# Four tokens of q and k to a partition, on half the partitions each, and a new order of all steps

## The chip, the cores and the metric

The kernel runs on one core of one Trainium2 chip. The time is that of one execution on the device, in microseconds (us), and the smaller the better. Before the change it is 206.74 us, the median of three runs that lie between 206.2 and 206.82 us.

## The reference, cut to what matters

Chunked attention over 8 batches, 8 heads, 576 tokens and a head width of 64 is followed by a phase-mixing layer of width 512. Attention stays inside chunks of 64 tokens.

```
q_c, k_c, v_c = (B, H, 9, 64, 64) views of q, k, v
scores = q_c @ k_c^T / 8;  attn = softmax(scores);  x = attn @ v_c     # (8, 576, 512)
theta = x @ w_theta
zr, zi = x * cos(theta), x * sin(theta)
y = einsum('ts,bsd->btd', w_tok_r, zr) + einsum('ts,bsd->btd', w_tok_i, zi)
u = x + y
out = u + max(u @ w_ch, 0)
```

The products with w_tok mix all 576 tokens of a batch, so a row of y needs z of its whole batch.

## The kernel before, in words

The batches are taken in four pairs (p = 0 to 3). A pair has 1152 tokens, cut into five groups: A and B are tokens 0 to 255 and 256 to 511 of its first batch, C and D the same of its second, and M is the 64 last tokens of both. A, B, C and D are "whole" groups of 256 tokens, M has 128.

Each group passes these steps, whose letters stand in the list `ORDER` at the top of the file as letter, optional half of the heads (0 or 1), pair, group, and PSUM banks: `q`, `k`, `v` load (`load_qk`, `load_v`, from the GpSimd queue, since the load turns float32 into float16); `L`, `T`, `N` turn q and k so that the head width lies on the partitions (`qk_t`, transposes on TensorE into PSUM); `tq`, `tk` copy them out of PSUM (`qk_copy`; A is ScalarE, V is VectorE); `S` scores, `e` exponent, `V` attention times v with a column of ones for the sum, `n` division; `X`, `Q` turn x and `xA`, `xV` copy it; `H` is x @ w_theta, `g` cos and sin (with the table loads `pg` and `pe` around it), `z` the two products; `Y` mixes the tokens (`YA`, `YC` and so on take the z of one group at a time), `y` adds x; `U`, `R` turn u, `W` is u @ w_ch, `w` the rest, `s`, `sA` store from the SyncE or ScalarE queue. `lt`, `lw`, `lc` load the weights, `TW` turns the token weights, `D.n` is n products of zeros whose result nobody reads.

The schedule is written out by hand: `tc.manual_schedule()` runs through `ORDER`, and each engine gets its instructions in that order and runs them in that order, waiting where data isn't there. Nothing else reorders the work. The GpSimd loads take turns on eight semaphores, so a load waits until the load eight places before it has landed. The first load of the next pair also waits, through `gate` (line 169), for a recent division.

A whole group of q is loaded by one transfer (line 197) as two tokens to a partition on 128 partitions: for each partition and head it reads two neighbouring tokens, 128 floats, and writes 256 bytes. That is 1024 pieces. k is loaded in the same way beside it. The turning has three forms. `L` ("long") takes 32 transposes of 128 partitions by 64 columns (line 305). `T` ("small") takes 64 transposes of 64 by 64 (line 318), and puts them on the four quadrants of the array. `N` ("plain") serves M. For x and u, `X` and `U` are 8 transposes of 128 by 128 (line 438) for 256 tokens, and `Q` and `R` are 32 of 64 by 64 (line 447).

v is loaded by three transfers for a whole group, one on all partitions and two on half of them (line 221), in pieces of 128 bytes, 2048 in all.

Of the kernel before, what the change touches and what calls it, by code (L numbers as in the profile page):

```python
# [10 lines left out]
FP16 = mybir.dt.float16  # L11
# [10 lines left out]
pg.00 g0.0B H1.0B.0 X1.0A.1 X0.0A.5 xA0.0A xA1.0A n1.0M g1.0B TW.00.3 H0.0A.2 g0.0A n0.0M X.0M.5  # L22
xV.0M TW.01.6 z0.0B H1.0A.5 H.0M.0 twA.01 q.0C z1.0B k.0C L.0C.1.2 twV.00 YB.0A.6 z0.0A g1.0A
z1.0A g.0M tq.0C YA.0A.6 lw.02 z.0M tkA.0C TW.02.0 YM.0A.6 S.0C.2 pe.00 e.0C twV.02 q.1A k.1A
y.0A L.1A.4.5 TW.03.0 tkA.1A q.0D k.0D v.0C L.0D.2.3 tkA.0D tq.1A S.1A.6 e.1A V0.0C.4 v.1A v.0D
lc.00 twV.03 YA.0B.0 V1.0C.6 q.1D n0.0C tq.0D S.0D.2 n1.0C k.1D YM.0B.0 lw.04 U.0A.4 X.0C.5 e.0D
uA.0A V1.0D.6 V0.0D.2 n1.0D YB.0B.0 V0.1A.6 xA.0C n0.0D V1.1A.2 n1.1A n0.1A H.0C.4 W.0A.2 Q.0D.6
y.0B xV.0D T.1D.0 pg.00 g.0C X.1A.4 tkA.1D U.0B.5 w.0A q.1C k.1C z.0C H.0D.6 q.1B xA.1A H.1A.2
uA.0B g.0D W.0B.4 YC.0D.6 g.1A q.1M tq.1D S.1D.0 pe.00 e.1D w.0B k.1B T.1B.4 tkA.1B T.1C.2 z.0D
tq.1C YD.0D.6 tkA.1C k.1M v.1B N.1M.0 TW.04.1 twA.04 YM.0D.6 z.1A S.1C.2 tkA.1M q.2A tq.1B y.0D  # L30
e.1C tq.1M k.2A S.1B.4 v.1D Y.0M.1 v.2A e.1B y.0M T.2A.6 V0.1D.4 V1.1D.2 YC.0C.0 q.2D YM.0C.0
v.1C k.2D tq.2A tkA.2A v.1M S.2A.6 e.2A n0.1D V0.1B.4 n1.1D sA.0A n0.1B V1.1B.2 n1.1B YD.0C.0
y.0C V1.1C.6 S.1M.4 e.1M q.3C X.1D.2 q.2B k.2B q.2M xA.1D X.1B.3 U.0C.0 n1.1C V0.1C.4 V0.1M.1
n0.1M V1.1M.2 q.2C uA.0C k.2C H.1D.6 W.0C.0 n0.1C X.1C.4 xV.1B n1.1M X.1M.5 pg.00 g.1D xA.1C
w.0C H.1B.2 V0.2A.0 v.3M v.2D z.1D xA.1M n0.2A q.3D g.1B V1.2A.6 n1.2A H.1M.4 g.1M z.1B U.0M.5
H.1C.0 uA.0M v.3D g.1C Q.2A.6 T.2B.2 z.1M Y.1A.4 q.3A z.1C Y.1D.0 tkA.2B xA.2A tq.2B Y.1C.2 k.3C
y.1D y.1A y.1C S.2B.0 pe.00 e.2B T.2C.6 T.2D.4 tq.2C tkA.2D tkA.2C v.2M k.3A R.0D.2 tq.2D k.2M
Y.1B.0 uA.0D v.2C v.2B N.2M.2 V0.2B.6 q.3M y.1B tkA.2M tq.2M S.2D.4 e.2D k.3D n0.2B Y.1M.3
S.2M.0 V1.2B.4 n1.2B S.2C.6 W.0M.2 e.2M V1.2M.0 e.2C Q.2B.4 xA.2B y.1M w.0M s.0M V0.2M.1 n0.2M
H.2A.6 R.1A.4 n1.2M V1.2C.0 H.2B.2 q.3B uV.1A pg.00 g.2A n1.2C Q.2M.0 xV.2M T.3D.4 tq.3D R.1B.6  # L40
W.1A.0 g.2B H.2M.2 s.0B z.2A v.3C s.0C w.1A s.1A uA.1B z.2B k.3B U.1C.3 W.0D.6 g.2M W.1B.0 uA.1C
tkA.3D w.0D s.0D z.2M V1.2D.2 w.1B sA.1B R.1D.6 n1.2D uA.1D Y.2A.4 S.3D.6 V0.2D.0 W.1D.2 y.2A
pe.00 e.3D R.1M.4 n0.2D uV.1M w.1D T.3B.0 tkA.3B tq.3B Q.2D.6 Y.2B.4 xA.2D v.3B V0.2C.6 S.3B.0
y.2B n0.2C H.2D.2 sA.1D k.3M e.3B V0.3B.0 n0.3B V1.3B.4 n1.3B W.1C.6 w.1C X.2C.0 pg.00 g.2D
W.1M.1 T.3C.2 w.1M xA.2C Q.3B.4 V0.3D.6 H.2C.0 tkA.3C n0.3D N.3M.6 xA.3B tq.3C g.2C H.3B.4 g.3B
z.2D tq.3M R.2B.2 tkV.3M z.2C V1.3D.0 n1.3D z.3B Y.2C.6 y.2C S.3M.0 uA.2B S.3C.2 pe.00 e.3M
# [13 lines left out]
def kernel(  # L60
# [186 lines left out]
    def cast_theta(a, copy):  # L247
        copy(out=wtheta16[:, 2 * a : 2 * a + 2], in_=wraw[a])
# [35 lines left out]
    def qk_t(p, g, f, form, *banks):  # L284
        n = 1 if g == "M" else 2
        ne, e0 = part(f)
        t = nats[p, g]
        if form != "small":

            if n == 2:  # L290
                pss = [psum(b, 1, FP16)[:, 0 : ne * n * P] for b in banks]
# [35 lines left out]
    def qk_copy(p, g, f, which, how):  # L327
        ps = st[p]["ps_qkT", g, f][which]
        _, nx, n, c = ps.shape
        name = "qk"[which] + "T"  # L330
        t = tmp.tile([P, nx, n, c], FP16, name=name, tag=f"{name}{n}")
# [12 lines left out]

    def scores(p, g, f, bank):
# [7 lines left out]
        for cc in range(n):  # L353
            for e in range(ne):
                for h in range(2):
                    for r in range(2):
                        x, r0 = (r * ne + e, 0) if form == "small" else (e, r)
                        k0 = (n * r0 + cc) * CH
                        i0 = r0 * CH + cc * CH // 2
                        kc = kf[half[h], x, k0 : k0 + CH]  # L360
                        if n == 1 or form == "plain":
# [4 lines left out]
                        nc.tensor.matmul(ps[to], kc, qc)  # L366
        st[p]["ps_sT", g, f] = ps

    def exps(p, g, f):
# [8 lines left out]
            )  # L378
            return
        if st[p]["form", g, f] != "plain":  # L380
            ps = ps.rearrange("p x (s i) -> p x i s", s=2)
        nc.scalar.activation(  # L382
            out=eT.rearrange("p h r e c -> p (h r e) c"), in_=ps, func=AF.Exp, scale=scale
        )
# [314 lines left out]
    def store(p, g, f, queue):  # L699
# [112 lines left out]
```

## Time and profile before

| what | value |
|---|---|
| median of three runs | 206.74 us |
| the profiled execution's own time | 205.98 us |
| its span | 204.2 us |
| TensorE (PE) busy | 192.3 us, 94% |
| VectorE (DVE) busy | 126.0 us, 62% |
| ScalarE (ACT) busy | 115.6 us, 57% |
| GpSimd (POOL) busy | 89.3 us, 44% |
| queue of the GpSimd loads | 81264 packets, 16.01 MB |

The span is what the profile covers; 1.8 us of the execution lie around it. "PE" rows are products and transposes, "PEld" the weight loads that run beside them. A row's time before an instruction is idle time of its engine, and the name behind the arrow is what ended it; "issue" means that the profile shows nothing that the engine waited for.

### The profile page before, as it was taken

The page shows a single profiled execution, that of the slowest core. Times are in us where ns is not written, and L with a number is a line of the kernel's source. Part 1 is how long each engine was busy: PE and PEld are TensorE (multiplying, and loading weights), DVE is VectorE, ACT ScalarE, POOL GpSimd, SP SyncE. Part 2 cuts the span into 40 slices and gives each one's busy share as a digit, 9 for nine tenths or more (in the row PEclk, how much of TensorE's full clock was granted, in tenths as well). Part 3 has the DMA queues.
Part 4 walks back from the last instruction along what each step waited for, and adds up shares of the span by engine and source line. Part 5 has one row for each costly group of instructions (what it writes and reads, how often), then busy time and mean ns, then how long its engine had stood idle before and what let it go on. Part 6 is the DMA issues. An engine that isn't in the chain of part 4 may idle for free.

```text
span 204.2 us, 7908 instructions
## 1 busy us (share of the span) xinstructions
PE 192.3 (94%) x3584; PEld 102.8 (50%) x3584; DVE 126.0 (62%) x226; ACT 115.6 (57%) x142; POOL 89.3 (44%) x130
## 2 busy tenths in 40 slices
PE   7977999999997799999999999999999999999991
PEld 2344556656464365544654645445555544454440
DVE  0335696667364587924467886589666768643662
ACT  2044996678985378960759836498960857030120
POOL 7889495649989289999403502230400000000000
PEclk9999999999999999999999999999999999999997
DMA  6999999999999989999904993940723002042546
GB/s 210 144 150 150 179 190 169 146 181 118 169 170 157 114 158 176 167 173 159 122 11 127 214 256 135 157 27 3 51 59 106 3 3 104 0 167 108 190 177 185
DMA packets 87009, 27.00 MB, mean 132 GB/s; under 512 B 80064, under 2 KB 81984, under 8 KB 86976
## 3 DMA queue, kind: packets, MB, share of 16 engines
q0 software_dynamic: 81264, 16.01, 93.2%
q1 hardware_dynamic: 3920, 7.08, 10.2%
q10 hardware_dynamic: 1792, 3.41, 4.6%
q8 instruction: 28, 0.46, 0.9%
q14 instruction: 5, 0.04, 0.0%
HBM read 33.06 MB, written 9.44 MB: 208 GB/s over the span
## 4 chain that ended last, share of the span: by engine, by line
PE 76%; DMA 13%; POOL 5%; issue 4%; DVE 0%; DVEq 0%; POOLq 0%
PE ps L564 29%; PE ps L478 27%; DMA v<-in_v_dram 7%; DMA qk<-in_k_dram 4%; PE ps L550 4%; PE ps L438 3%; PE ps L318 3%; PE ps L400 3%; PE ps L447 3%; POOL qk L197 3%; PE ps L366 2%; DMA out_dram<-o 1%; POOL v L221 1%; POOL wnat L232 1%; PE ps L301 1%
## 5 line engine op out<-in xcount | busy, mean ns | idle before, releaser
L564 PE MATMUL ps<-z,wT 128*128 128x512 f16 x288 | 65.6, 380 | 1.5 <-issue 1.5
L564 PEld LDWEIGHTS <-wT 128*128 128x128 f16 x288 | 26.9, 98 | 32.6 <-issue 1.8
L221 POOL DMA_DIRECT2D v<-in_v_dram x48 | 36.2, 766 | 7.0 <-DMA qk<-in_k_dram 3.3
L683 DVE TENSOR_TENSOR x<-ps,x 128x1024 f16<-128x1024 f32 (+1 forms) x22 | 22.5, 1028 | 25.2 <-PE ps L564 22.4
L478 PE MATMUL ps<-wtheta,xT 128*128 128x512 f16 x144 | 34.4, 380 | 0.1
L478 PE MATMUL ps<-wch,uT 128*128 128x512 f16 (+1 forms) x148 | 34.1, 374 | 0.0
L382 ACT ACTIVATE eT<-ps 128x1024 f16<-128x1024 f32 (+1 forms) x18 | 16.6, 928 | 25.8 <-PE ps L366 24.4
L693 DVE SCALAR_TENSOR_TENSOR o<-ps,x 128x1024 f32<-128x1024 f32 (+2 forms) x23 | 22.5, 990 | 10.7 <-PE ps L478 6.6
L461 ACT COPY uT<-ps 128x1024 f16<-128x1024 f16 (+1 forms) x16 | 14.4, 909 | 25.5 <-PE ps L447 12.5
L414 DVE TENSOR_TENSOR x<-ps,recip 128x512 f16<-128x512 f32 (+1 forms) x40 | 25.5, 638 | 1.4
L338 ACT COPY kT<-ps 128x1024 f16<-128x1024 f16 (+1 forms) x18 | 16.4, 927 | 15.9 <-PE ps L305 10.8
L492 ACT ACTIVATE cos<-ps,pihalf 128x1024 f16<-128x1024 f32 (+1 forms) x22 | 21.2, 965 | 6.1 <-PE ps L478 3.5
L169 POOL COPY seen<-recip 1x1 f32<-1x1 f32 x13 | 2.7, 210 | 45.9 <-DVE recip L412 45.9
L478 PEld LDWEIGHTS <-uT 128*128 128x128 f16 x148 | 13.7, 98 | 15.0 <-issue 0.4
L478 PEld LDWEIGHTS <-xT 128*128 128x128 f16 x144 | 12.9, 98 | 13.8 <-issue 0.2
L496 ACT ACTIVATE sin<-ps 128x1024 f16<-128x1024 f32 (+1 forms) x22 | 19.2, 873 | 0.0
L334 DVE COPY qT<-ps 128x1024 f16<-128x1024 f16 (+2 forms) x23 | 12.9, 569 | 6.4 <-PE ps L305 4.4
L197 POOL DMA_DIRECT2D qk<-in_q_dram x16 | 14.5, 905 | 2.3 <-issue 1.5
L412 DVE RECIPROCAL recip<-ps 128x8 f32<-128x8 f32 (+1 forms) x40 | 7.9, 197 | 12.2 <-PE ps L400 10.3
L197 POOL DMA_DIRECT2D qk<-in_k_dram x16 | 14.4, 900 | 1.0 <-issue 0.6
L137 ACT ACT_TABLE_LOAD x11 | 14.1, 1283 | 0.2
L461 ACT COPY xT<-ps 128x1024 f16<-128x1024 f16 (+1 forms) x13 | 11.8, 922 | 1.3 <-PE ps L447 1.0
(52 smaller groups left out, 204.5 us busy)
## 6 DMA issues: line engine op xcount, KB each, us to landing
qk<-in_q_dram POOLq DMA_DIRECT2D x16, 256.0 KB, 6.4
qk<-in_k_dram POOLq DMA_DIRECT2D x16, 256.0 KB, 6.5
out_dram<-o SPq DMA_DIRECT2D x8, 512.0 KB, 3.6
out_dram<-o ACTq DMA_DIRECT2D x6, 512.0 KB, 3.3
v<-in_v_dram POOLq DMA_DIRECT2D x40, 64.0 KB, 5.5
v<-in_v_dram POOLq DMA_DIRECT2D x16, 128.0 KB, 6.2
wraw<-in_moe_w_theta_dram SPq DMA_DIRECT2D x2, 512.0 KB, 3.8
out_dram<-o SPq DMA_DIRECT2D x8, 128.0 KB, 2.3
```

The costliest lines, as they stand in the source:

```text
L197: nc.gpsimd.dma_start(t.rearrange("p (h x) -> p h x", h=H)[:, hs], ap[2 * p + bb, :, s0 : s0 + GT, :].rearrange("h (p s) d -> p h (s d)", ...
L221: nc.gpsimd.dma_start(v16[rows, slot + tile, :, 0:D], v[2 * p + bb, :, t0 : t0 + m, :].rearrange("h s d -> s h d"),)
L338: nc.scalar.copy(out=t.rearrange("p x s c -> p x (s c)").rearrange("p x (c s) -> p x c s", s=2), in_=ps.rearrange("p x s c -> p x c s"),)
L382: nc.scalar.activation(out=eT.rearrange("p h r e c -> p (h r e) c"), in_=ps, func=AF.Exp, scale=scale)
L414: nc.vector.tensor_tensor(out=tokens(p, g, "x")[:, :, f * NE * D : (f + 1) * NE * D].rearrange("p c (h d) -> p c h d", h=NE), in0=psv[:, 0 ...
L461: (nc.vector.tensor_copy if how == "V" else nc.scalar.copy)(out=to.rearrange("p b (r c) -> p b r c", c=CH), in_=psv)
L478: nc.tensor.matmul(ps[:, a * DM : a * DM + cols.stop - cols.start], xT[:, b0 + a, db, :], weight[:, db, cols], start=(db == 0), stop=(db = ...
L492: nc.scalar.activation(out=cos[:, 0:n].rearrange("p a e -> p (a e)"), in_=pin, func=AF.Sin, bias=pihalf, scale=1.0,)
L496: nc.scalar.activation(out=sin[:, 0:n].rearrange("p a e -> p (a e)"), in_=pin, func=AF.Sin)
L564: nc.tensor.matmul(ps[:, a * DM : a * DM + DM], wT[:, kt, t0 : t0 + P], zs[bb], start=(done + k == 0), stop=(done + k == NK - 1),)
L683: nc.vector.tensor_tensor(out=u, in0=ps, in1=u, op=ALU.add)
L693: nc.vector.scalar_tensor_tensor(out=o, in0=ps[:, 0 : n * m].rearrange("p (j d) -> p j d", j=n), scalar=0.0, in1=u, op0=ALU.max, op1=ALU.add,)
```

## The change

Whole groups of q and k are loaded with four neighbouring tokens to a partition: q of the group on partitions 0 to 63, k on partitions 64 to 127 of the same tile. A piece is then 256 floats in and 512 bytes out, and a group of q has 512 pieces in place of 1024, and k the same. Two new forms of turning go with it. `F` ("four") takes 64 transposes of 64 by 64 on the four quadrants, for q and k together. `FL` ("four long") takes 32 transposes of 128 partitions by 64 columns, each of which turns q and k of one head at once. M is loaded as before. The copy of q may now run on ScalarE too (`tqA`). The copy of k puts its tokens back in natural order, and the scores pick q in steps, four at a time.

The whole list `ORDER` is new. In pair 0 the groups come as C, B, A, D, M instead of B, M, A, C, D; q and k of all groups and v of C are loaded ahead of the other v, and the token weights `lw` behind all of it. For whole groups, `L` in five groups (two of them by halves of the heads) and `T` in eleven become `FL` in six groups (two by halves) and `F` in ten; M of pair 0 is turned by `L` in place of `N`. `Q` and `R` (small) give way to `X` and `U` in part. The table loads `pe` and `pg` go from 11 to 7. The products of zeros go from 42 to 43, 26 of them ahead of the first transpose instead of 31.

```diff
 ORDER = """
-q.0B k.0B init.00 D.12.0 lt.00 ctV1.00 ctV0.00 q.0M k.0M id.00 D.19.0 L0.0B.0.1 tkA0.0B
-L1.0B.7.6 tq1.0B N0.0M.5 tkV0.0M tkA1.0B q.0A N1.0M.1 tq0.0B S1.0B.6 tkV1.0M tq0.0M D.3.2
-S0.0M.2 e1.0B tq1.0M S0.0B.4 v.0B D.4.0 V1.0B.0 e0.0B e0.0M V0.0B.2 n0.0B k.0A S1.0M.6 D.4.5
-L1.0A.5.4 v.0M n1.0B L0.0A.3.2 tq1.0A e1.0M Q0.0B.0 tq0.0A tkA1.0A S1.0A.6 Q1.0B.4 tkA0.0A
-S0.0A.2 e1.0A e0.0A V1.0M.6 xV1.0B v.0A V0.0M.7 xV0.0B V1.0A.0 n1.0A V0.0A.4 lw.00 n0.0A H0.0B.2
...
+qF.0C kF.0C init.00 qF.0B kF.0B lt.00 id.00 D.12.0 D.14.0 F.0C.0.1 tqA.0C D.4.2 FL0.0B.2 tq0.0B
+tkA.0C S.0C.0 tkA0.0B FL1.0B.6 e.0C qF.0A ctV0.00 S0.0B.4 kF.0A tkA1.0B FL0.0A.2 v.0C tq0.0A
+qF.0D tq1.0B D.5.0 V1.0C.0 tkA0.0A e0.0B S0.0A.2 n1.0C V0.0C.4 FL1.0A.6 n0.0C D.3.0 X.0C.0 e0.0A
+tqA1.0A q.0M xV.0C tkA1.0A S1.0B.2 e1.0B S1.0A.6 e1.0A kF.0D FL.0D.4 tkA.0D k.0M L1.0M.0 tq1.0M
+L0.0M.1 tkV0.0M ctA1.00 v.0B tqA0.0M v.0A tkV1.0M tq.0D D.5.6 S.0D.6 V0.0B.4 V1.0B.2 S1.0M.0
+e1.0M e.0D v.0D V0.0A.0 n0.0B V1.0A.4 n1.0B n0.0A S0.0M.6 e0.0M n1.0A H.0C.2 X1.0A.0 lw.00
+xV1.0A v.0M X0.0A.1 V0.0D.4 xV0.0A lw.02 pg.00 g.0C V1.0D.6 H1.0A.0 g1.0A H0.0A.1 TW.00.2 qF.1C
...
 def load_qk
+        if plain is None:
+            t = nats[p, g][half[which]].rearrange("p a x -> p (a x)")
+            nc.gpsimd.dma_start(
+                t.rearrange("p (h x) -> p h x", h=H),
+                (q, k)[which][2 * p + bb, :, s0 : s0 + GT, :].rearrange(
+                    "h (p s) d -> p h (s d)", s=4
+                ),
+            )
+            return
...
 def qk_t
+        if form == "four":
+            t = t.rearrange("p a x -> p (a x)")
+            pss = [psum(b, 1, FP16)[:, 0 : ne * 4 * CH] for b in banks]
+            pss = [ps.rearrange("p (e s c) -> p e s c", e=ne, s=4) for ps in pss]
+            for e in range(ne):
+                for s in range(4):
+                    for w in range(2):
+                        for h in range(2):
+                            x0 = ((2 * (e0 + e) + h) * 4 + s) * D
+                            nc.tensor.transpose(
+                                pss[w][half[h], e, s],
+                                t[half[w], x0 : x0 + D],
+                                id16[half[w], half[w]],
+                            )
+        elif form == "four long":
+            form = "four"
+            t = t.rearrange("p a x -> p (a x)")
+            ps = psum(banks[0], 2, FP16)[:, 0 : ne * 4 * P]
+            ps = ps.rearrange("p (e s w c) -> p e s w c", e=ne, s=4, w=2)
+            for e in range(ne):
+                for s in range(4):
+                    for h in range(2):
+                        x0 = ((2 * (e0 + e) + h) * 4 + s) * D
+                        nc.tensor.transpose(
+                            ps[half[h], e, s].rearrange("p w c -> p (w c)"),
+                            t[:, x0 : x0 + D],
+                            id16,
+                        )
+            pss = [ps[:, :, :, w] for w in range(2)]
...
 def qk_copy
-        elif n == 1 or st[p]["form", g, f] == "plain":
+        elif which == 0 or n == 1 or st[p]["form", g, f] == "plain":
             nc.scalar.copy(out=t, in_=ps)
...
-                    "p x (c s) -> p x c s", s=2
+                    "p x (c s) -> p x c s", s=n
...
 def scores
+                        if form == "four":
+                            k0 = (2 * r + cc) * CH
+                            kc = kf[half[h], e, k0 : k0 + CH]
+                            qc = qT[half[h], e, :, k0 // 4 : k0 // 4 + CH // 4]
...
 parted = {
+        "qF": lambda p, g, f: load_qk(p, g, 0, None, f),
+        "kF": lambda p, g, f: load_qk(p, g, 1, None, f),
+        "F": lambda p, g, f, *banks: qk_t(p, g, f, "four", *banks),
+        "FL": lambda p, g, f, *banks: qk_t(p, g, f, "four long", *banks),
+        "tqA": lambda p, g, f: qk_copy(p, g, f, 0, "A"),
```

More of the change, by code (lines that the diff above doesn't have):

```diff
@@ L23 @@
[L23 to L46, printed above, removed]
@@ new lines @@
+e.2M y.1C S.2B.6 F.2C.2.3 tkA.2C tq.2C Y.1M.0 y.1M X.2A.5 S.2C.2 V0.2M.4 sA.0B v.2C e.2B kF.3B
+xA.2A n0.2M V0.2B.0 W.0C.6 V1.2M.4 n0.2B H.2A.0 e.2C w.0C s.0C V0.2D.2 n1.2M V1.2B.4 n1.2B
+W.1A.6 X.2M.4 n0.2D pg.00 g.2A v.3D xA.2M X.2B.0 w.1A V0.2C.2 xA.2B F.3B.1.5 tq.3B V1.2C.6 n1.2C
+n0.2C U.1C.4 U.1B.0 uV.1B X.2D.1 tkA.3B xA.2D H.2M.5 v.3M v.3B H.2B.6 g.2M W.1B.0 g.2B kF.3A
+uV.1C R.1D.2 uA.1D Q.2C.4 H.2D.6 xA.2C z.2A z.2M W.1C.2 s.1A k.3M z.2B g.2D w.1C H.2C.4 s.1C
+W.1D.2 g.2C w.1B F.3C.0.1 F.3A.4.5 w.1D z.2C tkA.3A S.3B.6 e.3B tq.3A Y.2B.2 tq.3C tkA.3C z.2D
@@ L56 @@
+R.2C.4 s.2B z.3D R.2D.6 uA.2D z.3C Y.3M.0 y.3B R.3B.2 R.3A.6 uA.3A w.2M Y1.3C.1 uV.3B s.1D y.3M
+W.2D.2 Y0.3C.0 y1.3C uA.2C y0.3C W.3A.4 U1.3C.0 W.2C.6 w.2D s.2D sA.2M U.3M.1 w.2C sA.2C W.3B.2
+w.3A sA.3A w.3B Y1.3D.7 y1.3D Y0.3D.4 sA.2A y0.3D uA.3M W.3M.1 w.3M uA1.3C R0.3C.6 R0.3D.4
+uV0.3C s.3B R1.3D.2 uA0.3D W1.3C.0 W0.3D.1 s.3M w1.3C s1.3C w0.3D s0.3D uA1.3D W1.3D.7 w1.3D
+s1.3D W3.3C.0 W2.3C.1 w3.3C sA3.3C w2.3C sA2.3C
 """.split()
@@ L287, in qk_t @@
         t = nats[p, g]
-        if form != "small":
+        if form == "four":
[27 more added lines that the diff above has]
+            pss = [ps[:, :, :, w] for w in range(2)]
+        elif form != "small":
             if n == 2:
@@ L330, in qk_copy @@
         name = "qk"[which] + "T"
-        t = tmp.tile([P, nx, n, c], FP16, name=name, tag=f"{name}{n}")
+        t = tmp.tile([P, nx, n, c], FP16, name=name, tag=f"{name}{min(n, 2)}")
         st[p][name, g, f] = t
@@ L359, in scores @@
                         i0 = r0 * CH + cc * CH // 2
-                        kc = kf[half[h], x, k0 : k0 + CH]
-                        if n == 1 or form == "plain":
+                        if form != "four":
+                            kc = kf[half[h], x, k0 : k0 + CH]
+                        if form == "four":
+                            k0 = (2 * r + cc) * CH
+                            kc = kf[half[h], e, k0 : k0 + CH]
+                            qc = qT[half[h], e, :, k0 // 4 : k0 // 4 + CH // 4]
+                        elif n == 1 or form == "plain":
                             qc = qf[half[h], x, k0 : k0 + CH]
@@ L380, in exps @@
         if st[p]["form", g, f] != "plain":
-            ps = ps.rearrange("p x (s i) -> p x i s", s=2)
+            s = 4 if st[p]["form", g, f] == "four" else 2
+            ps = ps.rearrange("p x (s i) -> p x i s", s=s)
         nc.scalar.activation(
```

31 lines of the change are left out of this document (21 added, 10 removed).

## The prediction

> **What bounds the kernel now.** First the page's busy times, then the chain of waits, which is PE at 76%. So I read TensorE's idle places.
>
> ```profile
> span 204.2 us, 7908 instructions
> PE 192.3 (94%) x3584; PEld 102.8 (50%) x3584; DVE 126.0 (62%) x226; ACT 115.6 (57%) x142; POOL 89.3 (44%) x130
> ...
> q0 software_dynamic: 81264, 16.01, 93.2%
> ...
> q8 instruction: 28, 0.46, 0.9%
> ```
>
> PE is full from 20 us on, but for one place. Its instructions in order of time show the start and that place (the bracket is idle time and its end):
>
> ```profile
> 1.20 8.28 PE L277 MATMUL ps<-zeros 128*128 128x512 f16 x31 [1.20 <-DVE pihalf L131]
> ...
> 10.85 0.86 PE L305 MATMUL ps<-id,qk 128*64 128x128 f16 x24 [0.96 <-DMA qk<-in_k_dram]
> ...
> 20.48 0.84 PE L400 MATMUL ps<-v,eT 64*64 64x65 f16 x48 [0.44 <-ACT eT L382]
> ...
> 63.06 0.29 PE L366 MATMUL ps<-qT,kT 64*64 64x64 f16 x13 [1.29 <-issue]
> ...
> 68.17 2.10 PE L564 MATMUL ps<-z,wT 128*128 128x512 f16 x9 [1.52 <-issue]
> ```
>
> The first 20 us go by the loads: PE works off zeros until q of the first group is in, and is idle for k. The two "issue" gaps are code. The trace has 28 reads of 16,384 bytes on the instruction queue, 256 instructions each; one begins at 60.6, the next at 65.8, and PE goes on 2.4 us after each begins, 128 matmuls apart. While loads fill the queues, 4.2 to 6.5 us pass from PE's entry into one such block until the next can run; PE had 4.1 and 3.7 us of work in these two blocks.
>
> Stretches with mostly one kind of load give the rates (last column: GB/s read and written, here written):
>
> ```profile
> 5.00:20.00 15.00, 12.35 (x248) 6.80 (x247) 5.66 (x14) 4.17 (x9) 13.15 (x19) 1.00 1.80 148
> 36.00:38.00 2.00, 1.88 (x82) 1.45 (x77) 0.95 (x2) 1.39 (x3) 1.63 (x3) 1.00 2.34 154
> 40.20:42.00 1.80, 1.80 (x52) 1.42 (x51) 0.83 (x3) 1.80 (x3) 1.50 (x3) 1.00 1.21 199
> 43.50:45.00 1.50, 1.50 (x38) 0.84 (x38) 0.89 (x4) 0.97 (x2) 0.00 (x0) 1.00 1.74 177
> ```
>
> 36 to 38 us is v (128-byte pieces), 43.5 to 45 q and k (256), 40.2 to 42 w_ch (1024): 154, 177 and 199 GB/s. The first column after the stretch is PE.
>
> **PE's own work.** Spacing from start to start, from the chain of waits:
>
> ```profile
> 65.42 0.64 PE ps L318 x64
> ...
> 75.19 3.56 PE ps L478 x16
> ...
> 81.14 0.38 PE ps L400 x32
> ...
> 85.35 11.76 PE ps L564 x54
> ...
> 98.60 0.27 PE ps L447 x32
> ...
> 162.88 0.55 PE ps L438 x8
> ```
>
> With 0.1 us for a change of tile shape (32 small ones take 0.27 or 0.38 us), that is 8.4 ns for a 64x64 transpose, score or attention product, 216 for 512 columns, 56 for a 128x128 transpose; L305's 32 take 1.0 us up to the next instruction, 31 each. Counts in both programs, by these prices:
> - 64x64 of q and k 704 to 640: -0.54 us
> - 64x64 of x and u 672 to 480: -1.61
> - 128x128 of x and u 120 to 168: +2.68
> - 128x64 of q and k 160 to 208: +1.49
> - 128x128 of M 32 to 24: -0.45
> - zeros 42 to 43: +0.22
> - changes of tile shape 95 to 99: +0.40
>
> Sum **+2.2 us**, all on PE: before's order adds up to 188.3 us, the new one to 190.5. The new forms have no row; I price them by L318 and L305, whose operand shapes they share. Should all 64x64 of `F` need a change of shape more per group, 10 x 0.1 = 1.0 comes on top; a gain from them I bound by 0.5.
>
> **What PE loses.** Before's last matmul ends at 199.6 (195.99 + 3.64), so 199.6 - 188.3 = 11.3 us are lost: 7.3 by 26.2 us (clock still low for the first six zeros 1.3, start 1.2, the loads and latencies the rest), 3.4 between 57 and 74 (2.8 are the two gaps), 0.6 later. From the last matmul to the end of the span, 4.6 us, nothing changes: four last columns, two stores.
>
> **The new start.** The queue's order decides. Before, the last piece of v of A landed at 20.8 us by the trace. Up to it 1.05 MB of q and k (5.9 us at 177 GB/s) and 0.92 MB of M and v (6.0 at 154) pass: 11.9 us, after a first packet at 4.7. So 4.2 us are lag: the last of the 16 engines ends about 2 us behind the middle one, and starts and landings cost the rest. In the new order v of A stands behind q and k of four groups (2.10 MB), M's (0.26) and v of C and B, with A's 0.79. The 0.26 + 0.79 take 6.8 us at 154. The 512-byte pieces have no row: their rate lies between 177 and 199, so 11.9 to 10.5 us; I take 190 (as close to one as to the other), 11.05. Then v of A is in at 4.7 + 17.9 + 4.2 = **26.8 us** (26.2 to 27.6 by the rate; 28.9 if the lag grows with the work; 25.0 if it shrinks to what it is at 50 us, under 0.5 from middle to last).
>
> PE reaches V0.0A with 16.9 us of order behind it: 43 zeros 9.29, 64 transposes of `F.0C` 0.54, 64 + 32 of `FL` 2.98, 16 of M 0.50, 136 scores 1.14, 64 attention products 0.54, X.0C 0.45, about 15 changes 1.5. So 26.8 - 16.9 = **9.9 us** are lost there, if what comes earlier is in time: F.0C about 10.4 (before's k at 10.85, the same bytes, issues 0.2 to 0.4 us shorter), FL0.0B 13, FL0.0A 16.5, FL.0D 22, none later than V0.0A needs. The zeros count as work in both orders.
>
> **Code in the new start.** PE's blocks 94 to 222, 222 to 350 and 350 to 478 matmuls hold only 3.9, 3.9 and 4.2 us. The block entered near 18.6 lets the next run at 22.8 to 25.1, that one the next at 27.7 to 31.6; PE wants them about 23.5 and 29.4. I take 0.4 here. The later blocks under load hold 9.7, 5.8, 7.9, 5.0, 5.8 and 7.6 us against 4.2 to 6.5, so I take 0.5 in place of before's 2.8. (The blocks with 3.5 and 4.4 us come past 110 us; there the trace shows 2 to 4 us from entry to readiness.)
>
> The Trainium skill, "Runtime: NRT & Kernel Launch", section "Instruction fetch mechanics", says that crossing a 16 KiB boundary is mostly hidden. The two gaps say that under load it is not; by the rule the 0.9 us here would go, and the sum be 207.9.
>
> **The rest.** POOL issues a q or k in 0.90 us; the same count of pieces (512) for half of v takes 0.68, so 32 x 0.22 = 7 us leave POOL, which idles 46 us at its gates: nothing. Loads of pair 1 stand 2 to 3 us ahead of PE by the same rates, so they cost nothing unless PE is 3 us early. ACT loses four table loads (4 x 1.28 + 4 x 0.2 = 5.9 us) and swaps copies with DVE one for one; both are under 62% and cost nothing, except that from H.0C on ACT has 12.4 us in a row (three pairs of cos and sin, two wT copies of 1.16, the table) that PE needs 13.5 us later: cover 1 us, and 1 us lost if it goes. SP carries only theta in the first half of the run, in both orders; moved stores have the same bytes and, but for the last two columns, a later one behind them.
>
> **Sum.** Lost: 9.9 + 0.4 + 0.5 + 0.3 at the end = 11.1 against 11.3, -0.2; work +2.2. That is +2.0 on the profiled execution (205.98), 208.0; the median stands 0.76 above it, so **208.8 us**.
>
> **Rivals.**
> - Wide pieces are fast (faster). Place: the first 25 us. If 512-byte pieces write faster than 199 GB/s, v of A comes earlier; from 258 GB/s on, 11.05 becomes 8.15 and the loss falls by 2.9, which beats the 2.2 of work and 0.6. At twice 190, PE waits for code next (pair 350 not before 22): loss 8, time 205.6. Against it: w_ch at 1024 bytes reaches 199, reading twice that in float32, and the first 2 us of the theta load, which isn't turned to float16, read and write 393.
> - The Trainium skill, "DMA: Bandwidth & Descriptors", section "Specifications", asks for 512 bytes at least for line rate, and names a read-modify-write below. By it this change would bring just that rival's gain; the rows show a slope of size alone, 154 to 177 to 199, and no step.
> - Code holds the start (slower still): each of the three short blocks takes 6.5 us from 11.6 on, so matmul 478 comes at 31.6 instead of 29.8: +1.8, 210.6, plus the ACT chain 211.6. For it: the block entered at 19.6 in before took 6.5.
> - Half of the partitions is slow (slower): at v's 154 GB/s the 2.10 MB take 13.6, +2.6: 211.4. Against it: at 36 to 38 us pieces for half and for all partitions pass at one rate.
> - The start doesn't matter (same): lag shrinks to 25.0, code is hidden: -1.8 - 0.9, 206.1 to 206.9.
>
> **Numbers.** Likeliest (207.4 to 210.0) 0.46; code 0.18; half partitions 0.08; same or nearly 0.14; wide pieces 0.10; the order's unseen waits, above 211, 0.04. A measurement here tells 0.3%, 0.6 us, from no change. Faster: 0.10 and half of the 0.14 = 0.17; same 0.11; slower 0.72. Range 205.8 to 211.5.
>
> **What would show it.** Right: PE busy about 2 us up with zeros alike; first transposes near 10.4 us; V0.0A near 27; gaps "issue" at 61 to 68 gone; DMA at 5 to 25 us writing 150 to 180 GB/s. Wrong: GB/s well above 200 there, or PE working without a break before 25 us; or "issue" gaps at 24 and 30 us that the sum has at 0.4.

## The result and the profile after

| | before | after |
|---|---|---|
| median of 9 runs of each | 206.74 us (205.49 to 207.67) | 208.1 us (207.44 to 209.07) |
| the profiled execution | 205.98 us | 207.44 us |
| its span | 204.2 us | 205.3 us |
| start of the last matmul | 199.35 us | 201.29 us |
| from there to the end of the span | 4.86 us | 4.04 us |

The changed kernel is slower, by less than 2%: the ratio is 1.0153, 95% interval 1.0119 to 1.0187, and the ratio of the medians is 208.1 / 206.74 = 1.0066. The first leaves out executions more than 1.5% above the quickest of their kernel and implies a mean of about 205.0 us for before (208.1 / 1.0153), less than the quickest of the nine in the table, so the medians are the safer measure of the size. Both are given below. 208.8 us was predicted.

The page's first lines, after:

```profile
span 205.3 us, 7582 instructions
...
PE 194.4 (95%) x3417; PEld 105.1 (51%) x3417; DVE 123.7 (60%) x223; ACT 114.8 (56%) x139; POOL 81.5 (40%) x128
```

PE does 167 matmuls fewer and is busy 2.1 us longer (192.3 before): the fewer and larger transposes cost more than the small ones that they replace.

PE's instructions in order of time, after, are to be compared with the same view of before. The bracket is idle time and what ended it:

```profile
1.19 7.37 PE L287 MATMUL ps<-zeros 128*128 128x512 f16 x26 [1.19 <-DVE pihalf L131]
...
9.67 0.69 PE L308 MATMUL ps<-id,qk 64*64 64x64 f16 x62 [0.96 <-DMA qk<-in_k_dram]
...
12.45 0.64 PE L323 MATMUL ps<-id,qk 128*64 128x128 f16 x16 [1.11 <-DMA qk<-in_k_dram]
...
14.22 0.32 PE L412 MATMUL ps<-qT,kT 64*64 64x64 f16 x16 [0.19 <-ACT kT L379]
15.32 0.64 PE L323 MATMUL ps<-id,qk 128*64 128x128 f16 x16 [0.78 <-DMA qk<-in_k_dram]
...
17.51 0.29 PE L447 MATMUL ps<-v,eT 64*64 64x65 f16 x13 [0.21 <-DMA v<-in_v_dram]
...
19.47 0.23 PE L412 MATMUL ps<-qT,kT 64*64 64x64 f16 x5 [1.58 <-issue]
...
23.69 0.24 PE L346 MATMUL ps<-id,qk 128*64 128x128 f16 x1 [0.26 <-issue]
...
26.44 0.62 PE L447 MATMUL ps<-v,eT 64*64 64x65 f16 x32 [0.55 <-ACT eT L422]
27.36 0.26 PE L412 MATMUL ps<-qT,kT 64*64 64x64 f16 x8 [0.29 <-ACT eT L429]
```

Three more rows of before belong beside those that the prediction shows:

```profile
12.00 0.27 PE L301 MATMUL ps<-id,qk 128*128 128x128 f16 x2 [0.29 <-DMA qk<-in_q_dram]
12.85 0.49 PE L301 MATMUL ps<-id,qk 128*128 128x128 f16 x6 [0.58 <-DMA qk<-in_k_dram]
...
19.57 0.22 PE L366 MATMUL ps<-qT,kT 64*64 64x64 f16 x4 [0.82 <-issue]
```

After, PE waits for three k loads (2.85 us together) and briefly for v (0.21), twice for code (1.84) and three times for ScalarE (1.03). Before, the start has 1.83 us of waits for loads, 0.82 for code and 0.44 for ScalarE. The last two waits for ScalarE are for PSUM banks, by the kernel's own list: `V0.0A` writes a bank that the exponent of M's scores has to read first, and the scores after it take the banks of group D's. The code gaps of before at 63 and 68 us have no counterpart: between 60 and 70 us PE is never idle. The stretches, after (the first column after the stretch is PE, the last GB/s read and written):

```profile
8.00:14.00 6.00, 3.93 (x135) 2.38 (x133) 0.88 (x2) 2.35 (x3) 2.76 (x5) 1.00 1.50 185
...
60.00:70.00 10.00, 10.00 (x156) 5.20 (x153) 7.84 (x16) 3.79 (x5) 3.62 (x7) 1.00 1.07 111
```

Set against the order's work at the prediction's prices, PE had lost 9.5 us when `V0.0A` began and 10.2 at `H.0C`, and 10.9 at the last matmul (201.29 - 190.4). Before had lost 7.2 at 26 us, 10.6 at 68 us and 11.1 at the end (199.35 - 188.2). So the change pays 3.0 us more at the start (1.2 for loads, 1.0 for code and 0.6 for ScalarE by the rows above), saves about as much later, and its 2.2 us of added work remain, less 0.8 us of a shorter end.

### The profile page after: what moved, and what is told of

It is laid out like the page before. It is cut to its first block, busy times and chain, and to the rows that moved or that the text cites. A ratio compares the mean times of both kernels' runs of the same rounds, so it can differ in the third digit from the quotient of the medians.

```text
span 205.3 us, 7582 instructions
## 1 busy us (share of the span) xinstructions
PE 194.4 (95%) x3417; PEld 105.1 (51%) x3417; DVE 123.7 (60%) x223; ACT 114.8 (56%) x139; POOL 81.5 (40%) x128
## 4 chain that ended last, share of the span: by engine, by line
PE 88%; DMA 8%; issue 2%; ACT 1%; DVE 0%; DVEq 0%; POOLq 0%
PE ps L611 31%; PE ps L525 31%; PE ps L485 5%; DMA v<-in_v_dram 4%; PE ps L597 4%; PE ps L447 3%; DMA qk<-in_q_dram 3%; PE ps L412 3%; PE ps L308 2%; PE ps L494 2%; PE ps L323 2%; PE ps L276 2%; PE ps L287 1%; PE ps L342 1%; ACT eT L429 0%
## 5 line engine op out<-in xcount | busy, mean ns | idle before, releaser
L525 PE MATMUL ps<-wtheta,xT 128*128 128x512 f16 x144 | 33.9, 379 | 0.0
L508 ACT COPY uT<-ps 128x1024 f16<-128x1024 f16 (+1 forms) x11 | 8.9, 818 | 22.9 <-PE ps L494 9.5
L525 PEld LDWEIGHTS <-xT 128*128 128x128 f16 x144 | 13.2, 98 | 14.3
L375 DVE COPY qT<-ps 128x1024 f16<-128x1024 f16 (+2 forms) x14 | 7.7, 561 | 16.0 <-PE ps L323 13.3
L459 DVE RECIPROCAL recip<-ps 128x8 f32<-128x8 f32 (+1 forms) x40 | 7.8, 195 | 10.9 <-PE ps L447 10.9
L377 ACT COPY qT<-ps 128x1024 f16<-128x1024 f16 (+2 forms) x9 | 7.7, 852 | 11.2 <-PE ps L308 8.2
L508 ACT COPY xT<-ps 128x1024 f16<-128x1024 f16 (+1 forms) x12 | 10.7, 910 | 5.5 <-PE ps L485 5.1
L169 POOL COPY seen<-recip 1x1 f32<-1x1 f32 x11 | 2.2, 198 | 27.9 <-DVE recip L459 27.9
L180 POOL DMA_DIRECT2D qk<-in_q_dram x16 | 11.1, 695 | 4.5 <-issue 1.0
L287 PE MATMUL ps<-zeros 128*128 128x512 f16 x43 | 11.7, 424 | 1.2 <-DVE pihalf L131 1.2
```

The costliest lines, as they stand in the source:

```text
L287: nc.tensor.matmul(psum(bank, 1), zeros[:, 0:P], zeros)
L508: (nc.vector.tensor_copy if how == "V" else nc.scalar.copy)(out=to.rearrange("p b (r c) -> p b r c", c=CH), in_=psv)
L525: nc.tensor.matmul(ps[:, a * DM : a * DM + cols.stop - cols.start], xT[:, b0 + a, db, :], weight[:, db, cols], start=(db == 0), stop=(db = ...
```

## The experiments

Each kernel was timed in five rounds beside the kernel before on the same chip. In the first four the median of before was 206.9 us, in the next four 206.1, and in the last four 206.28 (runs 9 and 10), 205.91 and 207.07, so kernels of different groups are compared by their ratios. "Work" is the order's matmuls at the prediction's prices, "lost" the start of the last matmul less the work up to it.

**1. The changed kernel again**, as the reference for its variants.

> The changed kernel itself, beside the parts below. Theory (work and start): TensorE has 2.2 us more work, loses about as much at the start and at code as before in all; 1 to 3.5 us over before, ratio 1.005 to 1.017. Rival (the loads themselves cost, half of the partitions each): the same here; it is told apart by the two next kernels.

Measured: 208.83 us (207.96 to 210.44), ratio 1.0196 [1.0121, 1.0271], ratio of medians 1.0093. The profiled execution lost 11.4 us; V0.0A began at 26.85 us; code gaps of 1.19 and 0.54 us stand at 19.6 and 24.1 us, after the same matmuls as in the first trace. The picture repeats to half a microsecond.

**2. The loads alone**: before's order, with the four-token loads and the two new forms.

```diff
-q.0B k.0B init.00 D.12.0 ... L0.0B.0.1 tkA0.0B L1.0B.7.6 ...   T.1D.0   T.1B.4   T.1C.2   T.2A.6
+qF.0B kF.0B init.00 D.12.0 ... FL0.0B.0 tkA0.0B FL1.0B.6 ...   F.1D.0.1 F.1B.4.5 F.1C.2.3 F.2A.6.7
```

> The order of before, with the four-token loads and their transposes in it and nothing else changed. Theory (work and start): the same count of transposes at the same prices, so no more work; a q or k passes in 1.36 to 1.40 us instead of 1.45, the first k lands about 1.2 us earlier than before, and the two code gaps at 61 to 68 us stay, shortened at most: 0 to -1.5 us against before, ratio 0.993 to 1.000. Rival (the loads cost): the loss of the change shows here, ratio 1.01 or more.

Measured: 207.61 us (205.94 to 208.81), 1.0118 [1.0041, 1.0195], medians 1.0034. The theory's gain is not there: 7.1 us were lost by 26 us, as in before. PE's instructions and the stretches of this run:

```profile
63.24 0.31 PE L412 MATMUL ps<-qT,kT 64*64 64x64 f16 x15 [1.54 <-issue]
68.89 0.21 PE L447 MATMUL ps<-v,eT 64*64 64x65 f16 x1 [2.34 <-issue]
```
```profile
30.00:56.00 26.00, 25.71 (x483) 14.99 (x482) 16.42 (x29) 19.96 (x22) 16.51 (x26) 1.00 1.46 147
56.00:80.00 24.00, 20.12 (x549) 11.53 (x548) 14.09 (x27) 12.78 (x17) 15.01 (x23) 0.93 1.38 135
```

The two code gaps grew from 2.8 to 3.9 us. The granted clock (the column ahead of the last two) has a mean of 0.93 in the stretch that holds them: it was 0.50 from 69.75 to 73.16 us, just behind the longer gap, and 1.00 around that, which makes 3.41 x 0.5 = 1.7 us more. The profiled execution is the longest of the six. Three of them have a mean clock of 0.981 to 0.990 and took 208.2 to 208.8 us, the other three 0.997 to 1.000 and 205.9 to 207.0. So the loads by themselves gain nothing where before's order wants them, and the loss of this execution is code and clock. The rival got the ratio, though not that of the medians, and not by slow loads on half of the partitions.

**3. The order alone**: the changed order with two-token loads (`F` to `T` or `L`, `FL` to `L`).

```diff
-qF.0C kF.0C init.00 qF.0B kF.0B lt.00 id.00 D.12.0 D.14.0 F.0C.0.1 tqA.0C D.4.2 FL0.0B.2
+q.0C k.0C init.00 q.0B k.0B lt.00 id.00 D.12.0 D.14.0 T.0C.0 tqA.0C D.4.2 L0.0B.2.3
```

> The new order with the loads and transposes of before (two tokens to a partition; L or T where FL or F stood). Theory (work and start): 2.2 us more work as in the change, and v of group A comes later by eight loads of some 0.08 us and by the 2.2 us that half the pieces saved at the landing of the first ones, 1 to 2 us in all: ratio 1.012 to 1.025. Rival (the loads cost): with the old loads the loss goes, ratio 1.000 to 1.005.

Measured: 210.09 us (209.21 to 211.53), 1.0246 [1.0186, 1.0306], medians 1.0154, as the theory had it. PE's instructions, run 3:

```profile
11.48 0.45 PE L358 MATMUL ps<-id,qk 64*64 64x64 f16 x32 [1.06 <-DMA qk<-in_k_dram]
...
27.68 0.42 PE L446 MATMUL ps<-v,eT 64*64 64x65 f16 x29 [0.70 <-DMA v<-in_v_dram]
```

The first k is worked on at 11.5 us instead of 9.7, and V0.0A waits for v itself, at 27.7 us. Work is 191.2 us (0.7 more), 13.2 us are lost (11.4 in run 1). No gap of this start is put down to code: PE reaches matmul 222 at 19.46 us, just when the changed kernel's code let it go on (19.47). The clock was 0.50 from 12.1 to 15.5 us. The four-token form is worth 1.3 us in the new order (210.09 - 208.83), of which 0.7 is TensorE's work and not the loads', and nothing in the old one.

**4. Without 17 products of zeros** (`D.4.2`, `D.5.0`, `D.3.0`, `D.5.6` left out; nobody reads their results).

> The changed kernel without the 17 products of zeros that stand between the first steps of pair 0 (the 26 ahead of them stay); the result does not depend on them. Theory (the start goes by the loads and the code): the 3.7 us of zeros only fill waiting; the time is that of the change within 0.7 us. Rival (the start goes by TensorE's queue): 2.5 to 3.7 us less than the change, ratio about 0.998 to before. If the idle places lower the clock instead, it is slower than the change by up to 2 us.

Measured: 209.0 us (207.87 to 209.63), 1.0189 [1.0136, 1.0242], medians 1.0101. Work fell by 4.0 us to 186.5 and the time did not. The stretches:

```profile
15.00:20.00 5.00, 2.92 (x71) 2.30 (x71) 2.18 (x6) 2.45 (x5) 3.55 (x5) 0.65 1.93 173
20.00:25.00 5.00, 3.82 (x119) 3.50 (x119) 2.07 (x5) 3.55 (x6) 4.94 (x8) 0.67 1.93 120
25.00:30.00 5.00, 4.15 (x108) 2.03 (x95) 3.31 (x8) 3.24 (x6) 4.55 (x8) 0.67 1.23 139
```

Run 1, the middle one of these stretches:

```profile
20.00:25.00 5.00, 4.46 (x111) 3.21 (x112) 2.50 (x7) 4.43 (x7) 5.00 (x8) 1.00 1.95 122
```

The zeros fill time that PE would wait for loads and code anyway, so taking them out removes no waiting; and without them the granted clock from 15 to 30 us is about 0.66, where run 1 has 1.00. It is no chance of one execution: the mean clock of this run's six executions is 0.975 to 0.982, that of run 1's 0.984 to 1.000.

**5. Before's order, four-token loads, less code**: run 2 with `FL` for `F` in groups 1B, 1C and 2A, 96 matmuls fewer.

```diff
-F.1B.4.5 ... F.1C.2.3 ... F.2A.6.7
+FL.1B.4  ... FL.1C.2  ... FL.2A.6
```

> The order of before with the four-token loads, and three of its groups (B and C of pair 1, A of pair 2, those turned between 56 and 66 us) turned by 32 wide transposes (FL) instead of 64 small ones (F): 96 matmuls and 96 weight loads fewer there, three quarters of a code block, for 3 x 0.45 = 1.35 us more work. Theory (code, and the clock after it): the gaps of 1.5 and 2.3 us between 61 and 69 us go or shrink under 1 us in all and the clock stays full there, so 1 to 3.5 us less than the loads alone, 204.5 to 206.5. Rival (the gaps are waits for loads that the profile doesn't show): the gaps stay and the work comes on top, 1 to 1.5 us more than the loads alone.

Measured: 207.23 us (205.88 to 211.17), 1.0067 [1.0025, 1.0108], medians 1.0055. The profiled execution is the longest of the twelve, so its places are read and not its sizes. PE's instructions:

```profile
85.14 0.19 PE L307 MATMUL ps<-id,qk 64*64 64x64 f16 x1 [1.59 <-issue]
...
118.02 1.71 PE L524 MATMUL ps<-wtheta,xT 128*128 128x512 f16 x4 [2.03 <-issue]
```

The gaps at 63 and 68 us are gone, and others come at 85 and 118 us. No gain over before or over run 2 followed (medians 1.0055 and 1.0034), so the theory got the gaps and missed the time. The gap at 85 us is no accident: runs 10 to 12, with the same three groups in a long form, have one at the same block bound, of 0.38 to 0.53 us. Whether that at 118 us belongs to this execution alone is open.

**6. More code in the start**: the changed kernel with its 13 long zeros after the first 30 turned into 104 short ones of about the same time.

```diff
-D.5.0  ... D.3.0  ... D.5.6
+D.40.0 ... D.24.0 ... D.40.6   # products of 128x16 instead of 128x512
```

> The changed kernel with the 5, 3 and 5 long products of zeros in the start replaced by 40, 24 and 40 short ones (16 columns) of about the same time in all: 91 more matmuls and weight loads, 0.7 of a code block, and no more work. Theory (code holds the start too): idle time marked issue moves to the block bounds 128 matmuls apart and grows to 3 to 5 us in all by 30 us; 0.9 us of waits behind v go in return: 1.5 to 3.5 us more than the change. Rival (the start goes by loads alone): within 0.5 us of the change.

Measured: 214.71 us (212.7 to 216.79), 1.0422 [1.0341, 1.0503], medians 1.0418: 3.2% or 6.7 us above run 1 by the medians' ratios, more than the theory's 1.5 to 3.5 us. PE's instructions and the stretches:

```profile
18.06 0.39 PE L287 MATMUL ps<-zeros 128*64 128x16 f16 x8 [2.86 <-issue]
...
23.70 0.32 PE L415 MATMUL ps<-qT,kT 64*64 64x64 f16 x8 [1.44 <-issue]
```
```profile
15.00:20.00 5.00, 2.14 (x85) 1.95 (x81) 1.65 (x6) 1.68 (x3) 3.43 (x5) 0.69 2.11 169
20.00:25.00 5.00, 3.56 (x90) 3.19 (x86) 1.33 (x2) 2.27 (x4) 4.79 (x8) 0.50 2.13 116
```

With the same loads and about the same length of work, 91 more instruction pairs make 4.3 us of "issue" idle on PE by 30 us in place of 1.7 to 1.8, right after matmuls 222 and 350, and the clock falls besides. V0.0A begins 2.4 us later than in run 1. The last matmul starts 5.9 us later: the clock, 0.66 from 30 to 35 us, costs another 1.7, and 1.7 are a code gap at 138 us, far behind the edit, of which this one trace cannot say whether it belongs to the edit. The code mechanism holds for the start, and its price is the gap and the clock after it.

**7. v later**: the load of w_ch (`lc`) moved ahead of v of B in the changed order.

> The changed kernel with the load of w_ch (512 KB, first needed after 55 us) put ahead of v of group B of pair 0 and nothing else moved: everything behind it lands some 2.6 us later (512 KB at 199 GB/s). Theory (the start goes by the loads): 1.7 to 2.8 us more than the change, first seen at the attention products of A. Rival (the start goes by code or by TensorE's queue): under 0.5 us more.

Measured: 209.7 us (208.01 to 211.45), 1.0203 [1.0136, 1.027], medians 1.0175. Run 1 has 1.0196 and 1.0093, so by the medians' ratios this is 0.8% or 1.7 us more, and by the others 0.1%; the times alone decide little. In the trace, the last piece of v of A landed at 27.9 us instead of 25.3, V0.0A began at 28.43 instead of 26.44, and 13.3 us were lost where the two traces of the changed kernel lost 10.9 and 11.4. That is the expected size (1.7 to 2.8), but PE's instructions show another path than v's landing:

```profile
18.00 0.23 PE L411 MATMUL ps<-qT,kT 64*64 64x64 f16 x5 [1.51 <-issue]
...
24.34 0.24 PE L345 MATMUL ps<-id,qk 128*64 128x128 f16 x1 [2.04 <-issue]
...
28.43 0.55 PE L446 MATMUL ps<-v,eT 64*64 64x65 f16 x32 [0.49 <-ACT eT L421]
```
```profile
25.00:30.00 5.00, 4.14 (x120) 2.26 (x119) 2.93 (x8) 1.90 (x4) 4.29 (x8) 0.71 1.74 145
```

At 18.00 us PE was 1.5 us ahead of the changed kernel's first trace (19.47), since the first loads, which the edit doesn't touch, landed some 1.1 us earlier in this execution. It lost that and 2.0 us more by V0.0A: 1.8 at the second code gap (0.26 us in the changed kernel), 0.3 at k of D, and about 1.3 by the clock after the gap. The read of that block on the instruction queue began at 21.9 us. In the other traces of the changed kernel's start (both of its own, and runs 3, 4, 6 and 8) it began at 20.3 to 21.3 us, although PE had entered the block before at 17.8 us in one and at 19.6 in another: entering earlier did not bring the code earlier. v itself is again in before PE asks for it, by 0.04 us. So more loads ahead make this start later, in this one trace through code and clock; that v of A's landing binds it is not shown.

**8. v first**: v of C, B and A ahead of q and k of D and M, and the first part of the token weights ahead of v of D, with the work on them moved along.

```diff
-... tq0.0A qF.0D tq1.0B ... tqA1.0A q.0M xV.0C ... kF.0D FL.0D.4 tkA.0D k.0M L1.0M.0 ... v.0B ... v.0A ...
+... tq0.0A v.0B tq1.0B ... tqA1.0A v.0A xV.0C ... e1.0A qF.0D kF.0D ctA1.00 V0.0B.4 V1.0B.0 ... lw.00 ...
```

> The changed kernel with its start put in another order: v of C, B and A ahead of q and k of D and M, the first token weights ahead of v of D, and the attention products of A and B and the first H ahead of the transposes of D; same work, same bytes. Theory (the start goes by the loads): the first token weights land 1.5 us earlier (one v less ahead of them), TensorE has work for the time before, and loses 8.5 to 9.3 us by there instead of 10.2: 1 to 2 us less than the change. Rival (code holds it): the same blocks in the same time, within 0.4 us of the change. If ScalarE, whose cos and sin come in a row, takes over: no gain or a loss.

Measured: 214.58 us (213.45 to 215.31), 1.0443 [1.0377, 1.0509], medians 1.0411. v of A was in at 21.7 us, 3.6 us earlier, and it gained nothing. PE's instructions:

```profile
34.25 0.78 PE L275 MATMUL ps<-id,wnat 128*128 128x128 f16 x10 [0.81 <-ACT sin L542]
37.31 1.04 PE L484 MATMUL ps<-id,x 128*128 128x128 f16 x8 [1.89 <-ACT wT L282]
```

ACT's chain of tables, cos, sin and wT copies came too late, 18.3 us were lost, and the clock was 0.68 at 20 to 25 us and 0.69 at 35 to 40. The theory missed, and the case that it named for ScalarE came true: this order pays on ACT more than it gains at v. Whether another order with v ahead would do better is not shown.

**9. The end alone**: the kernel before with its last two stores on ScalarE's queue, as in the changed kernel.

```diff
-w3.3C s3.3C W2.3C.0 w2.3C s2.3C
+w3.3C sA3.3C W2.3C.0 w2.3C sA2.3C
```

> The kernel before with nothing changed but the queue of the last two stores, ScalarE's in place of SyncE's (as the changed kernel has them). In the traces so far the stretch from the start of the last matmul to the end of the span is 4.83 and 4.86 us with the three last stores one after the other on SyncE, and 4.0 to 4.05 us with two of them on ScalarE. Theory (the queue of the stores is the cause): 4.0 to 4.1 us here too, ratio to before 0.994 to 0.998 (-0.4 to -1.2 us). Rival (the stretch is short because the other work around the changed kernel's end differs, say the last column's copy on another engine): 4.7 to 4.9 us, ratio 0.998 to 1.002.

Measured: 206.2 us (204.76 to 208.9), 0.9983 [0.9945, 1.0021], medians 0.9996. From the last matmul's start to the end: 4.74 us. The issues, run 9:

```profile
199.53 1.12 SPq L703 DMA_DIRECT2D out_dram<-o  x2
200.74 0.54 SPq L707 DMA_DIRECT2D out_dram<-o  x1
200.79 0.84 ACTq L707 DMA_DIRECT2D out_dram<-o  x2
```

The last store is issued 0.99 us after the last matmul's start, as against 0.93 in the changed kernel and 1.62 in before, and the end does not come earlier. The queue isn't the cause; the rival holds.

**10. The end and less code**: run 9 with `L` for `T` in groups 1B, 1C and 2A, with the two-token loads of before.

```diff
-T.1B.4   ... T.1C.2   ... T.2A.6
+L.1B.4.5 ... L.1C.2.3 ... L.2A.6.7
```

> As the run before it, and groups B, C and A of pairs 1, 1 and 2 turned by the long form with the two-token loads that the kernel before has (96 fewer matmuls than before, so the 128-matmul code blocks hold more work where the loads run). By the prices of the prediction the work is 1.45 us more; the two code gaps at 61 to 69 us (2.8 us) should go, and the tail is 0.8 us shorter. Theory (code gaps go when the blocks hold more work): ratio 0.985 to 0.995, 203.5 to 205.5 us. Rival (the gaps only move on to the next blocks under load, as in the run with the four-token loads and less code): ratio 0.998 to 1.006, with issue gaps of 1 us or more after 70 us.

Measured: 205.23 us (204.2 to 206.24), 0.995 [0.992, 0.998], medians 0.9949. PE's instructions and the stretch:

```profile
84.94 11.17 PE L563 MATMUL ps<-z,wT 128*128 128x512 f16 x51 [0.46 <-issue]
```
```profile
56.00:80.00 24.00, 24.00 (x513) 14.69 (x512) 17.44 (x33) 16.95 (x21) 20.33 (x30) 1.00 1.90 171
```

PE is never idle from 56 to 80 us, where run 2 lost 3.9 us and the profiled execution of before 2.8; one gap of 0.46 is left. Work is 1.46 us more, 9.0 us are lost instead of 11.1, and the last matmul starts 0.68 us earlier than in before. The gain of 0.5% is all this: the end is 4.78 us long, as in run 9, where the theory wanted it 0.8 us shorter. Runs 11 and 12, which have the same three groups turned so, repeat the gain (0.9953 and 0.9956). The theory on code holds, and its rival in a small part: the gap of 0.46 us is at a later block bound.

**11. M's store on the other queue as well**: run 10 with `sA.3M` for `s.3M`.

> The run with the new tail and less code, and the store of M of pair 3 moved from SyncE's queue to ScalarE's as well. In the traces with before's end, SyncE issues this store from 0.19 us before the start of the last matmul to 0.41 us after it, so that the store of half 0 of D, whose data is ready at 0.18 us, is issued at 0.50; in the changed kernel the last store of SyncE is issued at 0.16 us, and the span ends 4.0 us after that matmul started instead of 4.7 to 4.9. Theory (the crowd of whole stores on SyncE makes the long end): D's store is issued at about 0.2 us, and the end comes 4.3 to 4.5 us after the last matmul's start: 204.7 to 205.1 us, ratio 0.991 to 0.997 with the run before it at 0.995. Rival (the engines' drain of the bytes sets it, whichever queue issues): 4.7 to 4.8 us and the same time as the run before it, 205.2 us, within 0.3%.

Measured: 205.56 us (203.62 to 206.9), 0.9953 [0.9911, 0.9995], medians 0.9983. The store of D's half 0 is issued at 0.21 us after the last matmul's start, as the theory wanted, and the end comes at 5.07 us and not at 4.3 to 4.5. The stretch in which M's transfers pass, now from ScalarE's queue (the last column is GB/s):

```profile
199.20:200.70 1.50, 0.00 (x0) 0.00 (x0) 0.37 (x2) 0.00 (x0) 0.00 (x0) 1.00 0.95 179
```

The moment of the issue doesn't set the end; the transfers themselves are the candidate left.

**12. M's column earlier**: run 10 with M's column of u @ w_ch, its rest and its store ahead of D's first column instead of behind it.

```diff
-W1.3D.1 w1.3C uV.3M w1.3D W.3M.0 ... s1.3D w.3M s.3M w0.3D
+uV.3M W.3M.1 w1.3C w.3M W1.3D.0 ... s.3M w1.3D s1.3D w0.3D
```

> The run with the new tail and less code (205.23 us, 0.995), with the column of M of pair 3 ahead of the first column of D instead of behind it: product, rest and store (the store is two transfers of 64 partitions). In before's order M's two transfers are issued 0.71 and 0.19 us before the start of the last matmul, in the changed kernel 3.04 and 2.45 us before it; that is the one difference left, after the queue that issues was found not to matter, that could explain 4.0 against 4.7 to 4.9 us from that matmul's start to the end of the span. Theory (M's transfers, late and on half of the partitions each, hold up the last three): 4.0 to 4.3 us, a ratio 0.990 to 0.994, about 204.6 us. Rival (all the bytes of the last 4 us count alike, wherever M stands): 4.6 to 4.9 us, and a ratio within 0.3% of 0.995.

Measured: 205.23 us (203.88 to 207.43), 0.9956 [0.9907, 1.0005], medians 0.9911; 4.77 us from the last matmul's start to the end. The rival holds in this form: one column earlier is not enough. What the traces do show is what M's store costs. Two stretches of before, the first with M's two transfers of 64 partitions, the second with transfers of 128 (last two columns: busy share of the engines, and GB/s):

```profile
199.60:201.10 1.50, 0.02 (x1) 0.00 (x0) 0.60 (x2) 0.00 (x0) 0.00 (x0) 1.00 0.83 179
201.10:202.80 1.70, 0.00 (x0) 0.00 (x0) 0.00 (x0) 0.00 (x0) 0.00 (x0) 0.78 0.85 305
```

The same in the changed kernel:

```profile
199.30:200.80 1.50, 1.50 (x10) 0.66 (x8) 1.17 (x3) 0.29 (x1) 0.00 (x0) 1.00 0.84 187
200.80:203.90 3.10, 0.76 (x7) 0.43 (x5) 1.28 (x3) 0.00 (x0) 0.00 (x0) 1.00 0.91 332
```

At about the same busy share M's transfers move 179 to 187 GB/s and the others 305 to 332. The packets say the same: one of 2,048 bytes takes 132 to 168 ns on average in the half microseconds of before in which M's pass, and 84 to 88 ns around them. In before they fill 1.5 us right behind the last matmul; in the changed kernel they are 0.5 us ahead of it, since M's column is the third before D's last. The Trainium skill, "SBUF — State Buffer", section "Door 1: The DMA port swizzle (why `[64,N]` ≈ `[32,N]`)", says that partitions 0 to 63 reach half of the ports, and gives 196 GB/s for them against 328 for all 128 at 1 MiB; these stretches agree. Moved by one column (run 12) M's transfers only changed places with a column of D, and the engines still had work without a break up to the end. That M's place three columns ahead makes the changed kernel's 4.04 us was not run alone, so it stays argued.

## Why the prediction was right, and where its steps failed

The forecast of slower and its size held (208.8 against 208.1, or 208.83 in run 1), because its largest term held. Three of the smaller ones were off and cancelled in part, and that part is luck: in the start, v came 1.5 us earlier than forecast and code cost 1.4 us more.

- **PE's own work, +2.2 us: right.** The loss stays within 0.7 us from 28 us to the end, so the prices hold over 170 us of work, those of the new forms too. PE busy +2.1. No run changes this term alone; it rests on this account of two traces.
- **The sum of what PE loses, -0.2 us: right as a sum** (11.1 to 10.9 by starts of the last matmul), and wrong in its parts, as follows.
- **The new start, 9.9 us lost at V0.0A by v of A at 26.8 us: right in size (9.5), only half in cause.** v of A landed at 25.27. The rate of 190 GB/s was good: q and k of a group, 262 KB each, are in on the middle DMA engine 1.35 to 1.46 us apart from the second load on, 180 to 194 GB/s. The 4.2 us of lag was the term that was mis-sized: landing 1.5 us early leaves 2.7. The lag of the last DMA engine behind the middle one, at the first load of q, came out between 0.1 and 2.6 us over all traces, and at 0.8 us for v of A; before's 2 us was carried over as if it were fixed. What then held PE was k of C, B and A (2.85 us), code (1.84) and ACT's exponent (0.84); V0.0A had no load to wait for, in the profiled execution or, if barely, with later loads (run 7); only with the slower two-token loads does it wait for v (run 3). So the loads bind this start through k and through the code that comes behind them, and v is close behind.
- **Code in the start, 0.4 us: failed**, measured 1.84 (1.72 in run 1). Before's own start has 0.82 (the row at 19.57), which the prediction left among "the loads and latencies". The step let 4.2 to 6.5 us pass from the entry into a block until the next can run, and asked only for the blocks after 18.6 us. PE entered the block of matmul 94 at 12.45 us, and the next one could run 7.0 us later, at 19.47; PE wanted it at 17.9, 0.7 us before the step had it, since the loads of k came earlier than foreseen. Run 6 shows the mechanism with 4.3 us.
- **Later code, 0.5 us in place of 2.8: right in direction, better than said**: none after 30 us. Run 10 gets the same from three groups turned by a longer form, without the new order.
- **"Moved stores cost nothing", the end unchanged: failed**, by 0.8 us to the good. The step looked at bytes and the number of later stores, and not at M's transfers, which pass at little more than half the rate. That their place makes the 0.8 us is argued and not run.
- **POOL**: 0.695 us for an issue of a q where 0.68 was taken (0.90 before), 7.8 us less busy where 7 was taken, and nothing gained by it.
- **ACT's cover of 1 us**: PE waits 0.55 and 0.29 us for ACT's exponents just ahead of H.0C, so part of it was gone already there; run 8 shows what it costs when it goes.
- **"A measurement here tells 0.3%": too good.** The intervals of the experiments are 0.3 to 0.8% to either side.

The rivals: **wide pieces are fast** did not come. The Trainium skill, "DMA: Bandwidth & Descriptors", section "Specifications", would have line rate from 512 bytes on; the 180 to 194 GB/s here show no step over the 177 at 256 bytes of before, and lie below the 199 at 1024. But these loads lie on 64 partitions each, and a limit of such transfers near 190 would hide a step, so the two are not told apart. **Half of the partitions is slow**, in the sense of 154 GB/s, is out by the same rate. **Code holds the start** was right that code costs there, and at which blocks, and wrong on the sum: the first block took 7.0 us but the next 4.2, and matmul 478 came at 29.4 us and not at 31.6. v's earlier landing paid for the 1.8 us. **The start doesn't matter** had v of A at 25.0 us, as it nearly was, but its hidden code did not come; runs 3 and 7 show that the start matters.

On the fetch of code: the Trainium skill, "Runtime: NRT & Kernel Launch", section "Instruction fetch mechanics", has the crossing of a 16 KiB block mostly hidden. Gaps of 1.2 to 2.9 us in runs 1, 2, 5 and 6 say that while loads fill the queues it isn't; later, in the changed kernel's first trace, the rule agrees: from 30 us on no gap of PE is put down to code.

## What to carry to other kernels

Price an edit of a PE-bound kernel by PE's own rows first; that term was the surest, and the time that a better start or fewer transfers promise has to beat it. Count matmuls between code blocks where loads fill the queues: replacing small transposes by longer ones in just the places where the gaps stand (run 10) was worth 0.5% over before, and by the medians' ratios 1.2% over the changed kernel (0.9949 against 1.0066), with 1.46 us of work added; the same swap with another load layout gained nothing that shows over before (run 5), so it has to be read from that kernel's own trace. And look at transfers of 64 partitions near the end of a kernel: one column earlier gained nothing (run 12), three columns earlier is what the changed kernel has, and no run tried that alone.

## What was not expected of the hardware

- Idle stretches of PE can cost twice. In these traces the granted clock is 1.00 or 0.50 and changes on a grid of 3.41 us; the values between, as 0.66 or 0.93, are means over longer stretches. From the first rise of the clock to 198 us, over all fourteen traces, every grid stretch at 1.00 in which PE was idle for 1.7 us or more (eight of them) was followed by one at 0.50. With 1.2 to 1.6 us of idle time three of sixteen were, with less none. Products of zeros that only fill a wait held it at 1.00 (run 1 against run 4), and the times of the two are alike (208.83 and 209.0 us), so there the zeros cost nothing and gained nothing.
- Stores from 64 partitions pass at 179 to 187 GB/s where those from 128 pass at 305 to 332, from SyncE's queue or ScalarE's (run 11: 179).
- The lag of the last DMA engine behind the middle one at the start differs by 2 us between executions with the same first loads (1.6 and 2.2 us in two traces of the changed kernel, 0.1 in runs 4, 6, 7 and 8), which is more than this change is worth.
